# Seven left and seven right operands of the mixing, some moved by multiples of 32 bytes, so that all four pairs of addresses modulo 64 occur

## The chip, the core and the metric

The kernel runs on one NeuronCore of a Trainium2 chip. The time is what the device takes for one execution, in microseconds (us); before the change it is 2311.45 us, the median of two runs (2307.46 and 2315.44 us). A smaller time is better. TensorE (PE in the profile) multiplies: it holds a left (stationary) operand of 128 columns, which a weight load (PEld) brings in, and streams a right (moving) operand of up to 512 columns past it; both are read from the on-chip memory SBUF, and results go to PSUM. VectorE (DVE), ScalarE (ACT) and GpSimd (POOL) do elementwise work, and SyncE (SP) issues most DMA transfers.

## The reference, cut to what matters

A layer norm with modulation, an attention with a compressive memory over four segments, its output projection, a second modulated layer norm, and a two-layer MLP that mixes tokens. The change touches only the last part:

```python
h = _layernorm(x, axis=-1)                                  # (B, S, D)
u = jnp.einsum("bsd,sf->bdf", h, w1) + b1                   # (B, D, F)
u = _gelu(u)
y = jnp.einsum("bdf,fs->bds", u, w2) + b2                   # (B, D, S)
```

with S = 2048 tokens, D = 1024 channels, F = 3584, all in float32.

## The kernel before, in words

The first 1000 us or so are the attention (projections at lines 193 and 201, scores at 466 to 473, values at 495), then comes the output projection (`out_proj`, line 706), whose end overlaps the start of the mixing, and from about 1226 us to the end the mixing runs (`mix`, line 798). It has two matrix products, one with `w1` and one with `w2`.

Each product is cut into **units**, and each unit is a 2x2 block product that is done with seven block products instead of eight (sums and differences of blocks are formed ahead). For a unit, `prepare` (line 753) loads the four weight blocks (`wr`), and forms seven **left operands**, numbered q = 0 to 6. Each is a tile `sp` of 128 partitions x 2 x 512 float32r numbers, that is 4096 bytes in each partition: a high part (a rounded copy, made by ScalarE at line 120) and a low part (the remainder, made by VectorE at line 123). The seven tiles come from one tag with seven places, so each unit uses all seven, and a place is free again when TensorE has used it up.

The seven **right operands** stay in place for many units. `b_tile` (line 682) gives one place for each q, of 12288 bytes: three blocks of 2 x 512 numbers (high and low). In the product with `w1` these hold blocks 0 to 2 of the normed activations (`bA`), and block 3 (`bB`) lies in the tiles that later hold the sums; in the product with `w2` they hold up to three blocks of the hidden activations (`bU`). The product with `w1` has 2 phases x 14 units with 4 blocks, the one with `w2` 5 phases x 8 units with 3, 3, 3, 3 and 2 blocks. `load_b` (line 810) refills the right operands at the end of a phase.

`mix` does, for each q and each block, three matmuls of 128 x 128 by 128 x 512: high by high, high by low, low by high (left part first). They add up in a PSUM bank, and ScalarE (line 803) or VectorE (line 805) adds the result to the sums `cc` (product with `w1`) or `ac` (product with `w2`). So there are 28 units x 7 x 12 = 2352 matmuls in the first product and 2352 in the second, 4704 in all. Every matmul loads its left operand anew.

Where things lie is the sum of the sizes of what was placed before: a tile of 8 floats for each partition is 32 bytes. Three unused tiles of that size stand in the kernel already (`offset` at the head of the constants, `pad` and `pad2` in two pools of the attention). As the built program places them, every operand of the mixing is at an address that is 32 modulo 64; modulo 256 all left and right operands of the mixing and of the output projection are at 224. In the attention's projections, the activations `h` are at 224 modulo 256 and the weights `wv` and `wq` at 160. All blocks and parts inside a tile are multiples of 512 bytes apart, so a tile's address modulo 256 holds for all of it.

The order on each engine is chosen by a scheduler that models times when the kernel is built; PE may take matmuls of one product between those of another, as the two have different PSUM banks.

Of the kernel before, what the change touches and what calls it, by code (L numbers as in the profile page):

```python
# [7 lines left out]
F32 = mybir.dt.float32  # L8
F32R = mybir.dt.float32r
# [9 lines left out]
P = 128  # L19
# [25 lines left out]
def attention_and_mlp(ctx, tc, x, wq, wkv, wo, beta, w1, b1, w2, b2, c, wm_a, wm_b, out):  # L45
# [70 lines left out]
    def split(dst, src, hi_eng, lo_eng):  # L116

        hi, lo = dst[:, 0], dst[:, 1]
        if hi_eng is A:
            A.copy(hi, src)  # L120
        else:
            hi_eng.tensor_copy(hi, src)
        lo_eng.tensor_tensor(lo, src, hi.bitcast(F32), op=ALU.subtract)  # L123
# [482 lines left out]
    for g in range(2, NG):  # L606
        n = 8 * g - 13
# [5 lines left out]
    for j in range(32):  # L613
        n = ML0 + MLS * j
        later(n, lambda j=j: mod_fetch(j), n + 2, lambda r, j=j: mod_late(j, r), "V")
    plan(WO0 - 3, lambda: spread(gaw, 0))
    for i in range(8):
        n = WO0 + WOS * i
# [27 lines left out]
    for q in skp + [late, prj, paw]:  # L646
# [6 lines left out]
    b3, raws, sx = (ctx.enter_context(tc.tile_pool(name=n, bufs=1, side="right", reuse_waits="tile"))  # L653
                    for n in ("b3", "wr", "s1"))
# [15 lines left out]
    NPR = 7  # L670
# [11 lines left out]
    def b_tile(pool, nk, q, name):  # L682
        return pool.tile([P, nk, 2, 512], F32R, tag=f"B{q}", bufs=1, name=f"{name}_{q}")

    bA = [b_tile(b3, 3, q, "bA0") for q in range(NPR)]
    pair_h = {}

    def out_proj(tt):
# [61 lines left out]

    sp = ctx.enter_context(tc.tile_pool(name="sp", bufs=1, reuse_waits="tile"))

    def prepare(weights, nk):


        n = nk * P
        r = raws.tile([P, 4, 512], F32, tag="wr", bufs=2, name="wr")[:, :, 0:n]
        SY.dma_start(r, weights)
        a11, a12, a21, a22 = (r[:, i] for i in range(4))
        s1 = sx.tile([P, 512], F32, tag="s1", bufs=1, name="s1")[:, 0:n]  # L760
        ops = {}

        def operand(q, src):
            ops[q] = sp.tile([P, 2, 512], F32R, tag="sp", bufs=7, name=f"sp{q}")[:, :, 0:n]
            split(ops[q], src, A, V)

        def sum_1():
            V.tensor_tensor(s1, a21, a22, op=ALU.add)
            operand(1, s1)

        def sum_2():
            V.tensor_tensor(a21, a11, a21, op=ALU.subtract)
            V.tensor_tensor(a11, s1, a11, op=ALU.subtract)
            operand(2, a11)

        def sum_4():
            V.tensor_tensor(a12, a12, a11, op=ALU.subtract)
            operand(5, a12)

        return ops, [lambda: operand(0, a11), sum_1, sum_2, lambda: operand(3, a12), lambda: operand(4, a21), sum_4,  # L780
                     lambda: operand(6, a22)]
# [42 lines left out]
    def fourth(name):  # L824

        t = [y_tile(f"{name}_{i}") for i in range(4)]
        return [t[q // 2][:, 2 * (q % 2):2 * (q % 2) + 2].bitcast(F32R) for q in range(NPR)]

    first_unit = prepare(w1[0, 0], 4)
    for f in first_unit[1][:2]:  # L830
        f()
# [28 lines left out]
    def w2_unit(ph, g):  # L860
        k0, nk = sum(KP[:ph]), KP[ph]
        return prepare(w2[g, :, 512 * k0:512 * (k0 + nk)].rearrange("p (b n) -> p b n", b=4), nk)
# [12 lines left out]
    for u, (ph, g) in enumerate(units):  # L875
# [35 lines left out]
        if not last:  # L911
            unit = prepare(w1[units[u + 1]], 4)
# [10 lines left out]
        if ph == 0:  # L923
            SY.dma_start(pcd[g], cc)
            if g == NG1 - 1:
                bA, bB = [nxt[q][0] for q in range(NPR)], [nxt[q][1] for q in range(NPR)]
# [74 lines left out]
```

## Time and profile before

| what | us |
|---|---|
| median of two runs | 2311.45 |
| the two runs | 2307.46, 2315.44 |
| span of the profiled execution, first to last instruction | 2310.5 |
| PE busy in it | 2233.7 (97%) |
| PE busy with the mixing (line 798; bU, bA, bB) | 536.3 + 434.5 + 164.6 |
| DVE busy | 1706.3 (74%) |
| ACT busy | 1105.9 (48%) |

How to read it: the profiled execution has no time of its own beside its span. The span lies 1 us below the median of the runs, and between the two of them, so the sum is made on the span and the 1 us is added. A matmul's duration in the trace (some 390 ns for 512 columns) is longer than the distance from one start to the next, since they overlap; what counts for the time is the distance from start to start. In a row of the timeline that stands for N matmuls in a row, that distance is the row's time less one duration, divided by N - 1.

### The profile page before, as it was taken

The numbers are of one execution on the slowest core, as the hardware profiler recorded it, in microseconds if no ns is written. First come the engines' busy times: TensorE is split into PE (matmuls) and PEld (weight loads), VectorE is DVE, ScalarE is ACT, GpSimd is POOL, SyncE is SP. The second block draws the span as 40 slices with busy tenths as digits, with TensorE's granted clock in tenths as the row PEclk, the third lists the DMA queues.
The fourth block names the chain that finished last, engine by engine and source line by source line (L and its number), as shares of the span: only waits on it lengthen the run. The fifth ranks groups of instructions, "written<-read, shape, count | busy, mean of one in ns | idle before, by whom it ended". The sixth has DMA issues, their size and how long they took to land.

```text
span 2310.5 us, 38455 instructions
## 1 busy us (share of the span) xinstructions
PE 2233.7 (97%) x13866; PEld 1920.3 (83%) x13866; DVE 1706.3 (74%) x3814; ACT 1105.9 (48%) x2018; POOL 724.2 (31%) x835
## 2 busy tenths in 40 slices
PE   8999999999999999988999999999999999999998
PEld 7879888888998888877777888888887888888887
DVE  6667666766776766666988565698889787878787
ACT  5477776665666666644323333443334242424232
POOL 3165565655666766653000000023333000000000
PEclk9989999999999999998999999999999999999999
DMA  6666564687566665663455755566557542414133
GB/s 256 199 171 190 168 176 147 193 253 252 162 204 180 196 182 164 185 202 109 137 196 192 268 222 188 200 228 232 208 203 259 186 140 66 150 56 141 55 119 146
DMA packets 172594, 414.67 MB, mean 179 GB/s; under 512 B 17236, under 2 KB 71540, under 8 KB 163444
## 3 DMA queue, kind: packets, MB, share of 16 engines
q1 hardware_dynamic: 167796, 403.83, 53.6%
q10 hardware_dynamic: 4608, 8.39, 1.0%
q8 instruction: 110, 1.80, 0.3%
q14 instruction: 80, 0.66, 0.1%
HBM read 236.23 MB, written 125.06 MB: 156 GB/s over the span
## 4 chain that ended last, share of the span: by engine, by line
PE 77%; DVE 10%; DMA 6%; ACT 3%; issue 2%; POOL 2%; SPq 1%; ACTq 0%; DVEq 0%; POOLq 0%
PE mx L798 41%; PE nps L193 11%; PE qps L201 8%; PE po L706 5%; PE pv L495 3%; DMA wr<-in_w_dram 1%; DVE ac L805 1%; PE a L466 1%; PE sx L431 1%; DVE bU L123 1%; DMA sk<-nt 1%; DMA x<-in_x_dram 1%; PE sz L431 1%; DVE sp L123 1%; DVE wv L123 1%
## 5 line engine op out<-in xcount | busy, mean ns | idle before, releaser
L798 PE MATMUL mx<-bU,sp 128*128 128x512 f32 x2352 | 536.3, 390 | 4.5 <-DVE ac L805 1.9
L798 PEld LDWEIGHTS mx<-bU,sp 128*128 128x128 f32 x2352 | 440.5, 188 | 99.7 <-DVE sp L123 2.7
L193 PE MATMUL nps<-wv,h 128*128 128x256 f32 x3072 | 437.2, 283 | 1.7 <-ACT wv L120 1.2
L798 PE MATMUL mx<-bA,sp 128*128 128x512 f32 x1764 | 434.5, 391 | 2.5 <-DVE sp L123 2.2
L120 ACT CAST sp<-wr 128x384 fp32r<-128x384 f32 (+2 forms) x408 | 216.8, 545 | 441.4 <-PE mx L798 368.0
L481 POOL TENSOR_TENSOR ph<-p,ph 128x640 f16<-128x640 f32 x256 | 377.6, 1496 | 149.9 <-ACT ph L479 144.1
L193 PEld LDWEIGHTS nps<-wv,h 128*128 128x128 f32 x3072 | 404.2, 189 | 7.8 <-ACT wv L120 1.4
L798 PEld LDWEIGHTS mx<-bA,sp 128*128 128x128 f32 x1764 | 332.6, 189 | 73.8 <-DVE sp L123 3.0
L123 DVE TENSOR_TENSOR sp<-wr,sp 128x384 fp32r<-128x384 f32 (+2 forms) x408 | 258.0, 643 | 35.0 <-ACT sp L120 34.7
L805 DVE TENSOR_TENSOR ac<-mx,ac 128x512 f32<-128x512 f32 x280 | 189.3, 685 | 90.3 <-PE mx L798 89.6
L201 PE MATMUL qps<-h,wq 128*128 128x512 f32 x768 | 202.4, 410 | 0.8 <-DVE r L356 0.8
L706 PE MATMUL po<-wo,ots 128*128 128x512 f32 x768 | 184.6, 400 | 11.9 <-DVE x L709 4.1
L706 PEld LDWEIGHTS po<-wo,ots 128*128 128x128 f32 x768 | 147.6, 194 | 44.7 <-issue 4.3
L432 DVE CUSTOM_DVE_ANT_0 sx<-sx,mask 128x128 f32<-128x128 f32 (+1 forms) x256 | 109.7, 428 | 99.0 <-PE sx L431 96.9
L479 ACT CAST ph<-p 128x1280 f16<-128x1280 f32 x128 | 160.7, 1256 | 37.5 <-POOL p L477 36.2
L201 PEld LDWEIGHTS qps<-h,wq 128*128 128x128 f32 x768 | 146.4, 197 | 31.3 <-PE sx L431 0.8
L798 PE MATMUL mx<-bB,sp 128*128 128x512 f32 x588 | 164.6, 389 | 0.0
L477 POOL TENSOR_SCALAR_AFFINE_SELECT p<-p 128x256 f32<-128x256 f32 x256 | 117.6, 469 | 142.4 <-ACT p L470 70.4
L495 PE MATMUL pv<-vp,ph 128*128 128x97 bf16 (+1 forms) x2560 | 146.2, 204 | 5.0 <-POOL ph L481 1.9
L495 PEld LDWEIGHTS <-ph 128*128 128x128 f16 x2560 | 116.4, 99 | 27.2 <-issue 7.9
L805 DVE TENSOR_TENSOR cc<-mx,cc 128x512 f32<-128x512 f32 x140 | 94.6, 683 | 51.0 <-PE mx L798 48.0
L798 PEld LDWEIGHTS mx<-bB,sp 128*128 128x128 f32 x588 | 110.6, 188 | 23.0
(173 smaller groups left out, 3199.8 us busy)
## 6 DMA issues: line engine op xcount, KB each, us to landing
sk<-sg SPq DMA_DIRECT2D x384, 128.0 KB
wr<-in_w_dram SPq DMA_DIRECT2D x28, 1024.0 KB
wr<-in_w_dram SPq DMA_DIRECT2D x32, 768.0 KB
bstu<-ucd SPq DMA_DIRECT2D x28, 768.0 KB
wsp<-wv SPq DMA_DIRECT2D x32, 512.0 KB
rawm<-in_wm_b_dram SPq DMA_DIRECT2D x32, 512.0 KB
wv<-wsp SPq DMA_DIRECT2D x32, 512.0 KB
pcd<-cc SPq DMA_DIRECT2D x14, 1024.0 KB
```

Source lines behind the costliest of these rows:

```text
L120: A.copy(hi, src)
L123: lo_eng.tensor_tensor(lo, src, hi.bitcast(F32), op=ALU.subtract)
L193: T.matmul(ps[:, aa], h[:, j, 128 * tt:128 * tt + 128], wt[:, i, o:o + 256], start=(n == 0), stop=(n >= 6 * NK - 2), skip_group_check=True)
L201: T.matmul(ps, wt[:, i, o:o + 128], h[:, j], start=(k + n == 0), stop=(3 * k + n == 3 * NK - 1))
L432: marks[4 * t + h - LEADS, "V"] = V.tensor_tensor_reduce(o, o, mask[:, 384 - 128 * i:], 1.0, -3.0e38, op0=ALU.add, op1=ALU.max, accum_out= ...
L477: G.affine_select(w, w, pattern=[[0, 2], [1, 128]], compare_op=ALU.is_ge, fill=0.0, base=0, channel_multiplier=-1)
L479: marks[n, "A"] = A.copy(ph[:, 0], p32)
L481: marks[n, "G"] = G.tensor_tensor(ph[:, 1, c], p32[:, c], ph[:, 0, c], op=ALU.subtract)
L495: T.matmul(pv[:, i, 0:w], ph[:, part, o:o + 128], d["vp"][:, j, h, 0:w], start=(n == 0), stop=(n == 19), skip_group_check=True)
L706: T.matmul(ps, os_[:, i, P * ct:P * ct + P], wop[ct, nh][:, j], start=(n == 0), stop=(n == 3 * NK - 1))
L798: T.matmul(ps, ops[q][:, i, P * k:P * k + P], b[:, j], start=(m == 0 and first), stop=(m == 3 * nk - 1), skip_group_check=True)
L805: V.tensor_tensor(d, ps, d, op=ALU.add)
```

## The change

Unused tiles of 32 bytes are put between some operands. Each right operand is followed by one, but for q = 3 (and the last); each left operand q gets a place of its own (`sp0` to `sp6`, in this order) in place of seven places under one tag, with an unused tile after q = 1 and after q = 4.

```diff
-    bA = [b_tile(b3, 3, q, "bA0") for q in range(NPR)]
+    bA = []
+    for q in range(NPR):
+        bA.append(b_tile(b3, 3, q, "bA0"))
+        if q in (0, 1, 2, 4, 5):
+            b3.tile([P, 8], F32, name=f"gapb{q}")
...
     sp = ctx.enter_context(tc.tile_pool(name="sp", bufs=1, reuse_waits="tile"))
 
+    spt = lambda q: sp.tile([P, 2, 512], F32R, tag=f"sp{q}", bufs=1, name=f"sp{q}")
+    for q in range(NPR):
+        spt(q)
+        if q in (1, 4):
+            sp.tile([P, 8], F32, name=f"gaps{q}")
+
...
         def operand(q, src):
-            ops[q] = sp.tile([P, 2, 512], F32R, tag="sp", bufs=7, name=f"sp{q}")[:, :, 0:n]
+            ops[q] = spt(q)[:, :, 0:n]
             split(ops[q], src, A, V)
```

No instruction of the computation is added, removed or given another size. The addresses in the built program, modulo 64 and (in brackets) modulo 256, and the matmuls of each:

| q | left `sp` | right `bA`, `bU` | matmuls with these | right `bB` | matmuls with `bB` |
|---|---|---|---|---|---|
| 0 | 32 (224) | 0 (64) | 588 | 32 (32) | 84 |
| 1 | 32 (224) | 32 (96) | 588 | 32 (32) | 84 |
| 2 | 0 (0) | 0 (128) | 588 | 32 (32) | 84 |
| 3 | 0 (0) | 32 (160) | 588 | 32 (32) | 84 |
| 4 | 0 (0) | 32 (160) | 588 | 32 (32) | 84 |
| 5 | 32 (32) | 0 (192) | 588 | 32 (32) | 84 |
| 6 | 32 (32) | 32 (224) | 588 | 32 (32) | 84 |

Before, all of these are 32 (224). What lies beyond moves along: the weight blocks `wr` and the sum `s1` go from 32 to 0 modulo 64, the sums `ac` and `cc` stay at 32. The built order of instructions is the same up to the start of the mixing; from there PE, DVE, ACT and SP take the same work in a somewhat different order, since the scheduler now has one place for each q.

## The prediction, on record before the run

> **What bounds the kernel now.** I read the page's first part, then the table of stretches for the mixing's line (798), then PE's timeline inside single stretches.
>
> ```profile
> span 2310.5 us, 38455 instructions
> PE 2233.7 (97%) x13866; PEld 1920.3 (83%) x13866; DVE 1706.3 (74%) x3814; ACT 1105.9 (48%) x2018; POOL 724.2 (31%) x835
> ...
> L798 PE MATMUL mx<-bU,sp 128*128 128x512 f32 x2352 | 536.3, 390 | 4.5 <-DVE ac L805 1.9
> L798 PE MATMUL mx<-bA,sp 128*128 128x512 f32 x1764 | 434.5, 391 | 2.5 <-DVE sp L123 2.2
> L798 PE MATMUL mx<-bB,sp 128*128 128x512 f32 x588 | 164.6, 389 | 0.0
> ```
>
> The three groups are all matmuls of the mixing: 2352 + 1764 + 588 = 4704. PE sat idle before them for 4.5 + 2.5 = 7.0 us in all. PE is thus the bound of the mixing, and with so little idle time any nanosecond that a matmul takes longer is paid at the end of the kernel.
>
> ```profile
> core 0: us, PE busy (x) PEld busy (x), PEclk, DMA share, GB/s
> 1350.00:1750.00 400.00, 400.00 (x1766) 331.32 (x1765) 1.00 0.56 209
> 1810.00:1900.00 90.00, 89.82 (x397) 73.97 (x396) 1.00 0.37 117
> ```
>
> At a granted clock of 1.00, 1766 matmuls start in 400 us: one each 226.5 ns. All operands are alike here (the same address modulo 256), and the spacing is the same in both products (90 / 397 = 226.7 ns).
>
> **What the address pair does in this trace.** The attention's query projection (line 201) has matmuls of the same form, 128 x 128 by 128 x 512 with high and low parts, but left and right lie 64 bytes apart modulo 128. Three rows of PE's timeline, one of the mixing first:
>
> ```profile
> start us, us, engine line op out<-in xcount [idle before <-releaser]
> 1502.12 2.20 PE L798 MATMUL mx<-bA,sp 128*128 128x512 f32 x9
> ...
> 665.57 3.60 PE L201 MATMUL qps<-h,wq 128*128 128x512 f32 x15
> ...
> 240.09 4.13 PE L201 MATMUL qps<-h,wq 128*128 128x512 f32 x17
> ```
>
> Less one duration (0.39, 0.39 and 0.40 us) and divided by one less than the count, the spacings are 226, 229 and 233 ns. No waits lie inside these rows. So the distance between the two operands is the most likely reason why equal matmuls take 2.8 or 6.6 ns longer than 226.5; that the stage differs in other ways (more ACT and POOL work beside it) speaks against it, but the spacing keeps the same value over a whole row while that work comes and goes.
>
> The output projection and the mixing also show what happens when a stream starts anew after a wait: the first matmuls are slower, then the spacing settles.
>
> ```profile
> 2119.50 1.77 PE L798 MATMUL mx<-bU,sp 128*128 128x512 f32 x7
> ...
> 2120.66 1.75 PE L798 MATMUL mx<-bU,sp 128*128 128x512 f32 x7
> ```
>
> The first row comes right after a wait, the second a microsecond later: seven matmuls cost 0.02 us more until they settle.
>
> **The change part by part.**
>
> *The gaps.* By the addresses of the built program, of 4704 matmuls 2604 have left and right at different addresses modulo 64 (q = 0, 3, 4, 5 with bA and bU: 4 x 588 = 2352; q = 2, 3, 4 with bB: 3 x 84 = 252). Another 756 agree modulo 64 but lie 64 apart modulo 128 (q = 6 with bA and bU: 588; q = 0, 1 with bB: 168). The remaining 1344 agree modulo 128, of which 588 have both at 0 (q = 2).
> - The 756 are like the query projection: +2.8 ns (its commoner value) makes 756 x 2.8 = 2.1 us; at +6.6 it is 5.0 us.
> - The 2604 have no like in the trace. From below: +0, or a gain (a rival, below). From above: the left operand's read no longer hidden, 60 ns (a rival, below). The nearest rows are the two of the query projection, and I take the larger, +6.6 ns, since a distance of half a 64-byte step should not fit better than a whole one: 2604 x 6.6 = 17.2 us. At 2.8 it is 7.3 us.
> - The 1344 I cost at nothing: they agree, as all do now.
> - Changes of the pair: in the built order of after, PE goes from one distance modulo 128 to another 645 times, against never before. Each may unsettle the stream as a restart does, 0.02 us: at most 645 x 0.02 = 12.9 us. A stretch between two changes has 4704 / 646 = 7 matmuls on average, and those with bB only three, which is too short to pay it in full: I take half, 6.5 us.
>
> *A place of its own for each q.* The operands are ready long before they are needed, because ACT waits for PE to free a place, not PE for ACT:
>
> ```profile
> engine line waited for: us in total, times, longest us
> ACT sp L120 <- PE mx L798: 440.6, 259, 5.0
> ...
> PE mx L798 <- DVE ac L805: 1.9, 3, 0.9
> PE mx L798 <- DVE sp L123: 1.7, 2, 0.8
> PE mx L798 <- ACT sp L120: 0.6, 1, 0.6
> ```
>
> (The first row is of all engines from 1300 us on, the others of PE from 1262 us on.) Seven places stay seven places, used in the same order; cost nothing. What hides it is the lead of nearly one unit, 84 matmuls x 226.5 ns = 19 us, in the first product; if it were gone, ACT's queue would stop at one place, and behind it the copies of results (line 803) that free PSUM.
>
> *The order at the start of the mixing.* The scheduler begins with three products at once where it had two.
>
> ```profile
> 1226.24 1.25 PE L798 MATMUL mx<-bA,sp 128*128 128x512 f32 x4 [0.28 <-ACT sp L120]
> 1229.71 3.36 PE L798 MATMUL mx<-bA,sp 128*128 128x512 f32 x7 [2.22 <-DVE sp L123]
> ```
>
> Here PE waits once for 2.2 us, and the seven matmuls after it stand (3.36 - 0.39) / 6 = 495 ns apart. Against 226.5 ns that loses 2.2 + 6 x 0.27 = 4 us. Another order may lose it twice or not at all: -4 to +4 us, taken as 0. Line 758's transfers move past others on SP's queue there, by one or two places; they wait for free buffers of wr, not for the queue.
>
> *DVE and ACT at other addresses.* Their tiles move too (wr and s1 to 0 modulo 64), and no row shows them there. DVE is the fuller one:
>
> ```profile
> 1300.00:1600.00 300.00, 300.00 (x1325) 248.51 (x1324) 213.06 (x293) 113.41 (x190) 26.66 (x17) 1.00 0.58 215
> 1600.00:1900.00 300.00, 297.90 (x1310) 245.21 (x1310) 252.20 (x376) 111.20 (x184) 64.27 (x39) 1.00 0.56 201
> ```
>
> (The third number after the window's length is DVE's, with its count.) DVE is busy for 213 and 252 of 300 us, so in the fuller stretch it could become 300 / 252 = 1.19 times as slow before it, and not PE, set the pace. Costed at nothing.
>
> **The sum.** 17.2 + 2.1 + 6.5 = 25.8 us: span 2310.5 + 25.8 = 2336.3, and with the 1 us to the median 2337 us (+1.1%). This case's own range: from 7.3 + 2.1 = 9.4 us (2321) to 17.2 + 5.0 + 12.9 = 35.1 us (2347).
>
> **The rivals.**
>
> *Not slower: a right operand at 0 modulo 64 is read in fewer pieces.* Shorter matmuls of the attention:
>
> ```profile
> 127.75 0.22 PE L472 MATMUL a<-sk 98*128 98x128 f32 x1
> 127.81 0.33 PE L473 MATMUL a<-sk 98*128 98x256 f32 x1
> ...
> 67.98 4.24 PE L193 MATMUL nps<-wv,h 128*128 128x256 f32 x36
> ```
>
> 128 columns take 60 ns, 256 take (4.24 - 0.28) / 35 = 113 ns. In steps of 113 / 17 = 6.65 ns that is 9 and 17 steps for 8 and 16 pieces of 64 bytes, one more than needed, as an operand has that starts in the middle of a piece; all these start at 32 modulo 64. At 0 the step would go: 588 x 3 = 1764 matmuls (q = 0, 2, 5) x 6.65 = 11.7 us less, 2300 us, if the unlike pairs cost nothing. Against it: 512 columns take 34 steps, two more than 32, which a cost in proportion to the length describes as well. It decides from the point where those products' spacing falls under 226 ns.
>
> *Much slower: the two reads get in each other's way all along.* If the streams are half a step apart, each of the nine pieces of a left operand (128 x 4 = 512 bytes, from the middle of a piece) could hold up the right one by half a step: 9 x 3.3 = 30 ns x 2604 = 78 us, 2389 us. The upper bound is a left operand's read not hidden at all, which the 60 ns above limit (a 128-column matmul with its own load): 156 us, 2467 us. It passes 2% from 46 / 2604 = 17.7 ns, a spacing of 244 ns. For it: the spacing of the mixing is as even as if both reads ran in step. Against it: the largest excess of any row here is 6.6 ns.
>
> *The change does nothing to the time.* The spacing follows from the column count alone, and the query projection's 229 and 233 ns come from its stage. The time stays at 2311 us. For it: rows of the same line show both 229 and 233 ns at the same addresses. Against it: both differ from the 226 ns of all rows with like addresses.
> The Trainium skill stands on this rival's side: "SBUF — State Buffer", section "Who interferes with whom", gives TensorE two independent read ports and says "PE and ACT never wait on anyone", and "TensorE: Matmul & The Clock Gate", section "Back-to-back issue gap", gives N / 2.4 + 2.5 ns, 216 ns for 512 columns, with no address in it. The trace does not agree with either in full: 226 ns is the least spacing of any 512-column row here, and 229 and 233 ns occur in equal matmuls without a wait.
>
> **How the numbers follow.** Chances: the sum above 0.45, much slower 0.33, not slower 0.12, nothing 0.10. The predicted time is the first one's, 2337 us. The range 2298 to 2390 us holds the first, the third and the fourth, and about half of the second; outside are the other half of that (0.16) and a little below (0.04). About 2% (46 us) is what a measurement of this kernel can tell from no change. Slower by more: the second case and a tail of the first, 0.34. Faster by more would need 10 ns off each of all 4704 matmuls, for which no row speaks: 0.01. Within 2%: 0.65.
>
> **What would show it.** In PE's timeline of after: spacings of q = 1 and 2 at 226 to 227 ns, of q = 6 at 229 to 233, of q = 0, 3, 4, 5 at 233. Were q = 0, 2 and 5 (with bA or bU) under 226, the first rival is right; were the unlike pairs over 244, the second. PE's idle time before line 798 should stay under 15 us, and DVE's mean for an addition at line 805 should stay at 685 ns:
>
> ```profile
> L805 DVE TENSOR_TENSOR ac<-mx,ac 128x512 f32<-128x512 f32 x280 | 189.3, 685 | 90.3 <-PE mx L798 89.6
> ```
>
> If either changes, the time has gone to the order or to DVE and the reasoning about addresses is not what decides.

## The result, and the profile after

The changed kernel takes 2336.74 us, the median of two runs (2335.95 and 2337.53 us), against 2311.45 us before: 1.0108 times as long, with a 95% interval of 1.0089 to 1.0127. It is slower by 25 us, which is clear of the scatter and under 2%. The prediction said 2337 us. The number is right, but of the terms that it is made of only the largest came out; the experiments show which others did not.

The page of the changed kernel (its line 808 is line 798 of before):

```profile
span 2334.2 us, 38446 instructions
PE 2257.6 (97%) x13866; PEld 1916.6 (82%) x13866; DVE 1709.4 (73%) x3814; ACT 1106.0 (47%) x2018; POOL 722.6 (31%) x835
...
L808 PE MATMUL mx<-bU,sp 128*128 128x512 f32 x2352 | 549.8, 395 | 2.4 <-DVE ac L815 1.7
...
L808 PE MATMUL mx<-bA,sp 128*128 128x512 f32 x1764 | 444.1, 396 | 3.1 <-DVE sp L123 1.9
...
L815 DVE TENSOR_TENSOR ac<-mx,ac 128x512 f32<-128x512 f32 x280 | 190.3, 686 | 96.8 <-PE mx L808 95.9
...
L808 PE MATMUL mx<-bB,sp 128*128 128x512 f32 x588 | 167.9, 394 | 0.2 <-DVE bB L123 0.2
```

The span is 23.7 us longer and PE is busy 23.9 us longer, with the same 13866 matmuls. The three groups of line 808 take 549.8 + 444.1 + 167.9 = 1161.8 us against 1135.4 us, 26.4 us more, and the other groups together 2.5 us less. PE's waits before them are 5.7 us against 7.0, and VectorE's addition stays at 686 ns (685 before). So neither a wait nor VectorE pays, the matmuls themselves do. The table of stretches for this line, with the same stretch as before:

```profile
core 0: us, PE busy (x) PEld busy (x), PEclk, DMA share, GB/s
1350.00:1750.00 400.00, 400.00 (x1720) 322.90 (x1719) 1.00 0.56 207
1850.00:2050.00 200.00, 200.00 (x860) 161.22 (x859) 1.00 0.35 110
```

1720 matmuls start in the 400 us that held 1766: one each 232.6 ns in place of 226.5, at the same granted clock of 1.00.

From the start times of single matmuls in the two traces, put beside the built order (which names q and so the addresses), the spacing by pair follows. Below, the distance is the left operand's address less the right one's, modulo 256; the mean leaves out spacings over 260 ns, which are waits, the one slow spacing after a wait (some 340 ns), and in before a stretch of some 427 ns each at a lower clock; a spacing is put down to the matmul that starts it; the last column is the count times what the mean lies over 226.67 ns.

```
distance   matmuls of after          count  mean ns  over 226.67, us
 96        q 3, 4, 5 with bA, bU     1764   233.7    12.4
160        q 0 with bA, bU            588   233.5     4.0
224        q 2, 3, 4 with bB          252   231.7     1.3
 64        q 6 with bA, bU            588   232.8     3.6
192        q 0, 1 with bB             168   231.7     0.9
128        q 1, 2 with bA, bU        1176   232.2     6.5
  0        q 5, 6 with bB             168   230.8     0.7
                                     4704            29.4
(before: distance 0, all 4704, 226.8 ns, 0.4 us)
```

Of these 29.4 - 0.4 = 29.0 us, 3.6 are given back by shorter stretches over 260 ns (13.1 us before, 9.5 after), and 1.4 as the mixing starts 1.4 us earlier: 24.0, and the span grew by 23.7 us. The time is thus accounted for. Most of the 3.6 us is one stretch: after its longest wait, before has 13 spacings of some 427 ns at a granted clock of 0.51, 13 x 0.2 = 2.6 us, and after has no such stretch. Before, then after:

```profile
1229.80:1236.00 6.20, 6.20 (x15) 4.90 (x16) 0.51 0.16 46
```

```profile
1229.80:1236.00 6.20, 5.98 (x25) 4.44 (x24) 1.00 0.22 54
```

Among the kernels of the experiments below, some with all pairs alike (e3) and some with unlike ones (e6, e9, e10, e12) have such a stretch early in the mixing, and others of both kinds have none. So these 2.6 us are chance as far as the traces tell, and no effect of the distance.

What stands out is that no pair kept its old spacing, not even the 1176 that agree modulo 128.

### The profile page after: what moved, and what is told of

Same layout as the page of the kernel before. It is cut to its first block, busy times and chain, and to the rows that moved or that the text cites. A ratio compares the mean times of both kernels' runs of the same rounds, so it can differ in the third digit from the quotient of the medians.

```text
span 2334.2 us, 38446 instructions
## 1 busy us (share of the span) xinstructions
PE 2257.6 (97%) x13866; PEld 1916.6 (82%) x13866; DVE 1709.4 (73%) x3814; ACT 1106.0 (47%) x2018; POOL 722.6 (31%) x835
## 4 chain that ended last, share of the span: by engine, by line
PE 78%; DVE 8%; DMA 5%; ACT 3%; POOL 3%; issue 2%; SPq 1%; ACTq 0%; DVEq 0%; POOLq 0%
PE mx L808 43%; PE nps L193 11%; PE qps L201 7%; PE po L710 5%; PE pv L495 3%; POOL ph L481 1%; PE a L466 1%; PE sx L431 1%; PE sz L431 1%; DMA x<-in_x_dram 1%; DMA sk<-nt 1%; PE up L413 1%; DMA wr<-in_w_dram 1%; PE a L469 1%; ACT ph L479 1%
## 5 line engine op out<-in xcount | busy, mean ns | idle before, releaser
L808 PE MATMUL mx<-bU,sp 128*128 128x512 f32 x2352 | 549.8, 395 | 2.4 <-DVE ac L815 1.7
L808 PE MATMUL mx<-bA,sp 128*128 128x512 f32 x1764 | 444.1, 396 | 3.1 <-DVE sp L123 1.9
L123 DVE TENSOR_TENSOR sp<-wr,sp 128x384 fp32r<-128x384 f32 (+2 forms) x408 | 264.2, 655 | 35.3 <-ACT sp L120 34.2
L808 PE MATMUL mx<-bB,sp 128*128 128x512 f32 x588 | 167.9, 394 | 0.2 <-DVE bB L123 0.2
```

Source lines behind the costliest of these rows:

```text
L808: T.matmul(ps, ops[q][:, i, P * k:P * k + P], b[:, j], start=(m == 0 and first), stop=(m == 3 * nk - 1), skip_group_check=True)
```

## The experiments

Three theories. **Distance** (called A in the expectations): the distance between left and right sets a steady spacing. **Changes** (called S): only going from one pair to another costs. **Pieces** (called F): a right operand at 0 modulo 64 is read faster. Ratios are to before, on the same chip.

**e1 and e2: one uniform distance of 32 with bA and bU, from either side.** The pairs with bB stay alike.

```diff
+    sp.tile([P, 8], F32, name="lead")       # e1: ahead of the left operands
...
+    b3.tile([P, 8], F32, name="tail")       # e2: after the right operands, which moves bA and bU down
```

> Before, with one unused tile of 32 bytes ahead of all left operands: every left operand is at 0 modulo 256, bA and bU stay at 224, bB moves to 0. So in the product with w2 all 2352 matmuls have one and the same unlike pair (left 0, right 32 modulo 64), with no change of pair. Theory A, that an unlike pair costs 6.6 ns steadily: spacing of bU 233 ns, and 4116 matmuls with bU and bA x 6.6 = 27 us, about 2339 us. Theory S, that only changes of the pair cost: spacing of bU 226.5 ns as before, and only the product with w1, which changes between bA and bB, pays some 6 to 12 us, about 2320 us. Theory F, that a right operand at 0 modulo 64 is read faster: nothing gained here, as the right operands with bA and bU stay, about 2311 us.

> Before, with one unused tile of 32 bytes after all right operands, which moves bA and bU to 192 modulo 256 (0 modulo 64); left operands and bB stay at 224. The mirror image of the run with the left operands at 0, at the same distance of 32 between left and right. Theory A: spacing of bU 233 ns, about 2339 us. Theory S: bU at 226.5 ns, about 2320 us. Theory F: 4116 matmuls x 6.65 ns less, spacing of bU 220 ns, about 2284 us.

Measured: e1 2339.94 us (1.0113, interval 1.0091 to 1.0135), e2 2337.76 us (1.0104, 1.0085 to 1.0123). The stretch from 1850 us, in the product with `w2`, of before, of e1, then of e2:

```profile
1850.00:2050.00 200.00, 199.82 (x882) 165.07 (x881) 1.00 0.35 111
```

```profile
1850.00:2050.00 200.00, 200.00 (x859) 161.01 (x858) 1.00 0.35 110
```

```profile
1850.00:2050.00 200.00, 200.00 (x858) 160.92 (x857) 1.00 0.34 108
```

Both start some 858 matmuls in 200 us, one each 233 ns, where before had 882 with a short wait among them. From the single starts, the mean with bU is 233.3 ns in both, and the same repeating row of 231, 232 and 235 ns. There is no change of pair in this product, so Changes falls as the main cause. In e2 the right operands are at 0 modulo 64 and no faster, so Pieces falls. Which of the two is moved makes no difference.

**e3: all operands at 0 modulo 256.**

```diff
+    sp.tile([P, 8], F32, name="lead")
...
+    b3.tile([P, 56], F32, name="tail")
```

> Before, with 32 bytes ahead of the left operands and 224 bytes after the right ones: all left operands, bA, bU and bB are at 0 modulo 256. All pairs are alike, as before, only at 0 in place of 32 modulo 64. Theory A (the distance decides): spacing 226.5 ns, about 2311 us. Theory S (changes decide): the same. Theory F (a right operand at 0 is read faster): 4704 x 6.65 = 31 us less, spacing 220 ns, about 2280 us.

Measured: 2312.65 us (0.9999, 0.9984 to 1.0015).

```profile
1350.00:1750.00 400.00, 400.00 (x1766) 331.24 (x1765) 1.00 0.55 210
```

The count is that of before to the matmul. 0 and 32 modulo 64 are equally good as long as left and right agree modulo 256.

**e4: places of their own, no gaps.** The changed kernel without its seven gap tiles.

```diff
-        if q in (0, 1, 2, 4, 5):
-            b3.tile([P, 8], F32, name=f"gapb{q}")
...
-        if q in (1, 4):
-            sp.tile([P, 8], F32, name=f"gaps{q}")
```

> After without any gap: each left operand has a place of its own, with the order of work that follows from it, and all addresses are those of before. Theories A, S and F all say 2311 us. The rival that the new order or the fixed places cost the time says up to 2337 us, with PE waits before line 798's matmuls of more than 15 us.

Measured: 2316.29 us (1.0009, 0.9993 to 1.0024), which is no difference that can be told; the spacing with bU is 226.8 ns. The other half of the edit, with the order that follows from it, is not the cause.

**e5 and e6: distances of 64 and 128 with bA and bU.** As e1, with `[P, 16]` and `[P, 32]`.

> Before, with 64 bytes ahead of the left operands: left at 32 modulo 256, bA and bU at 224, so every pair in them agrees modulo 64 but lies 64 apart; no change of pair in the product with w2. Theory D64 (only the distance modulo 64 counts): spacing of bU 226.5 ns, about 2312 us. Theory D128 or D256 (the distance counts modulo 128 or 256): 229 to 233 ns as in the query projection, 4116 x 2.8 to 6.6 = 12 to 27 us, 2323 to 2339 us.

> Before, with 128 bytes ahead of the left operands: left at 96 modulo 256, bA and bU at 224, 128 apart. D64 and D128: spacing of bU 226.5 ns, about 2312 us. D256: 233 ns, about 2339 us. In the changed kernel q = 1 and 2 lie 128 apart and run at 232 ns in their short stretches; if they settle at 226.5 here, their cost there came from the changes of pair, and if not, from the distance itself.

Measured: e5 2337.88 us (1.0108, 1.0088 to 1.0129), e6 2336.51 us (1.0106, 1.0087 to 1.0125). Stretches of e5, then of e6:

```profile
1350.00:1750.00 400.00, 400.00 (x1721) 323.06 (x1720) 1.00 0.55 205
1850.00:2050.00 200.00, 200.00 (x859) 161.47 (x858) 1.00 0.33 107
```

```profile
1350.00:1750.00 400.00, 400.00 (x1728) 324.60 (x1727) 1.00 0.55 205
1850.00:2050.00 200.00, 200.00 (x862) 162.07 (x861) 1.00 0.34 107
```

With bU, 233.3 ns at 64 and 232.4 ns at 128. So neither agreement modulo 64 nor modulo 128 is enough. The 232.2 ns of q = 1 and 2 in the changed kernel is what distance 128 costs for good, not an effect of the changes around them.

**e7: like and unlike pairs in turn.** e4 with one gap of 32 bytes after q = 3, so that with bU q = 0 to 3 are at distance 0 and q = 4 to 6 at 32.

```diff
     for q in range(NPR):
         spt(q)
+        if q == 3:
+            sp.tile([P, 8], F32, name="gap")
```

> The kernel with a place for each left operand and no gap, with one gap of 32 bytes after q = 3: with bU, q = 0 to 3 have like pairs (distance 0) and q = 4 to 6 a distance of 32, so the pair changes between stretches of 6 to 9 matmuls. If a change costs nothing, the like pairs stay at 226.5 ns and the unlike run at 233 ns, 2100 x 6.6 = 14 us, about 2328 us. If each change unsettles the stream, the like pairs lie at 229 to 232 ns too, 3 to 5 ns on 2604 matmuls = 8 to 13 us more, about 2340 us.

Measured: 2331.61 us (1.0085, 1.0067 to 1.0104), between the two expectations.

```profile
1850.00:2050.00 200.00, 200.00 (x870) 163.08 (x869) 1.00 0.35 111
```

From the single starts: bU at distance 0 runs at 228.2 ns, at 32 at 232.9; bA at distance 0 at 230.1. By place in a stretch at distance 0, the first eight spacings after a change have means of 228 to 232 ns, and from the ninth on it is 226.7 to 227.1. Added up, a change to distance 0 costs some 25 ns, close to the 0.02 us of a restart in the prediction. At distance 32 no such settling shows: the mean by place is 231 to 235 ns from the first spacing to the last. So in these traces a change costs only where there is a better spacing to settle into. The changed kernel agrees: at 96, 160, 64 and 128 with bA and bU its means are 233.7, 233.5, 232.8 and 232.2 ns, and without changes of pair (bU in e9, e10, e5 and e6) they are 234.3, 233.3, 233.3 and 232.4.

**e8: alike pairs in the attention's projections.** Before, with `pad2` larger:

```diff
-    acst.tile([P, 8], F32, name="pad2")
+    acst.tile([P, 24], F32, name="pad2")
```

> Before, with the unused tile pad2 of the attention 96 bytes in place of 32: the projection weights wv and wq move by 64 to 224 modulo 256, where the activations h are, so the projections' pairs become alike; the mixing stays as it was. If the distance decides there too, query projection rows settle at 226.5 ns in place of 229 and 233 and key/value rows at 113 in place of 113 to 118: at most 768 x 4 + 3072 x 2.5 = 11 us less, about 2300 us, and less where short stretches do not settle. If the stage and not the distance makes those rows slow: no change, 2311 us.

Measured: 2313.01 us (1.0001, 0.9991 to 1.0010). Its query projection and its key/value projection:

```profile
666.04 3.11 PE L201 MATMUL qps<-h,wq 128*128 128x512 f32 x13
```

```profile
69.57 4.24 PE L193 MATMUL nps<-wv,h 128*128 128x256 f32 x34
```

The queries settle at (3.11 - 0.39) / 12 = 227 ns, where before had 229 and 233: the distance decides there as well. But key/value, with 256 columns, now takes (4.24 - 0.28) / 33 = 120 ns where before had 113, at distance 64. What fits 512 columns does not fit 256. Over all key/value matmuls (spacings over 140 ns left out) the mean rises from 116.1 to 119.4 ns, some 10 us, and the queries give back one. Of these 9 us only 2.3 reach the start of the mixing (1228.51 us against 1226.24): PE's spacings over 260 ns ahead of it add up to 5.3 us less in this profile, and the rest is not accounted for. The kernel's time does not change, so this half of the expectation, the gain, is missed.

**e9 to e12: the other distances.** The same two edits in one kernel each, the lead ahead of the left operands 96, 160, 192 or 224 bytes and `pad2` 64, 128, 160 or 224.

```diff
+    sp.tile([P, 24], F32, name="lead")      # e9; e10: 40, e11: 48, e12: 56
...
-    acst.tile([P, 8], F32, name="pad2")
+    acst.tile([P, 16], F32, name="pad2")    # e9; e10: 32, e11: 40, e12: 56
```

> Two distances at once, left less right modulo 256: 96 in the mixing with bA and bU (96 bytes ahead of the left operands); in the projections, by pad2 of 64 bytes, 32 for key/value (256 columns) and 224 for queries (512 columns). If 0 is the only distance that fits for 512 columns, bU runs at 232 to 234 ns and the time is about 2338 us plus or minus what the projections change. If distances over 64 fit again, 226.5 ns. Key/value rows: 113 ns at 64 and some 119 ns at 0 so far; an unlike distance modulo 64 should be no better than 119, up to 10 us more for the kernel.

> Distance 160 in the mixing with bA and bU; in the projections, by pad2 of 128 bytes, 224 for key/value and 32 for queries. If 0 is the only distance that fits: bU at 232 to 234 ns, about 2338 us. If the distance counts the same both ways round, bU has the pattern and mean of distance 96. Query rows: 233 ns as in the mixing at 32.

> Distance 192 in the mixing with bA and bU, which is the query projection's own distance in the kernel before; in the projections, by pad2 of 160 bytes, 192 for key/value and 64 for queries. If the distance alone sets the spacing, bU shows the query projection's two values, 229 or 233 ns: 2352 + 1764 matmuls x 2.5 to 6.7, 2321 to 2339 us. Key/value: if 192 is to 256 columns what 64 is, 113 to 118 ns.

> Distance 224 in the mixing with bA and bU, 32 the other way round; in the projections, by pad2 of 224 bytes, 128 for key/value and for queries. If the distance counts the same both ways round, 233.3 ns as at 32, about 2339 us; if the order matters (the left operand read ahead of the right one), another value, 226.5 ns at the least. Key/value at 128: 113 ns if 64 fits because it is not 0, 119 ns if as at 0.

Measured: e9 2340.50 us (1.0117, 1.0100 to 1.0134), e10 2340.42 us (1.0124, 1.0104 to 1.0144), e11 2327.11 us (1.0059, 1.0037 to 1.0081), e12 2343.17 us (1.0120, 1.0096 to 1.0144). These times hold the changed projections as well, so the distances are compared by spacing. Two stretches of e11, and a row of its timeline:

```profile
1900.00:1950.00 50.00, 50.00 (x215) 40.50 (x216) 1.00 0.41 127
...
2150.00:2200.00 50.00, 50.00 (x220) 41.00 (x220) 1.00 0.20 64
```

```profile
2219.65 4.74 PE L799 MATMUL mx<-bU,sp 128*128 128x512 f32 x20
```

At distance 192 the mixing has the query projection's two values: 215 matmuls in 50 us are 233 ns, and the row of 20 is (4.74 - 0.39) / 19 = 229 ns. Another stage, other work beside it, the same distance, the same two values. All distances from the single starts, with bU for the mixing, and for the two projections the mean from the ninth matmul of a stretch on:

```
distance (left less right, modulo 256)     0     32     64     96    128    160    192    224
mixing, 512 columns, ns                226.8  233.3  233.3  234.3  232.4  233.3  229.9  233.3
queries, 512 columns, ns               227.2  233.3  233.3      -  232.6      -  229.6  233.3
key/value, 256 columns, ns             119.9  118.4  114.1      -  118.9      -  117.6  117.0
kernel                                before     e1     e5     e9     e6    e10    e11    e12
(key/value: 0 is e8, 32 e9, 64 before, 128 e12, 192 e11, 224 e10)
(queries: 0 is e8, 32 e10, 64 e11, 128 e12, 192 before, 224 e9)
```

The queries run in another stage, and their distance was set by another tile (`pad2`); at all six distances that were tried there, the two rows agree within 0.4 ns (at 192 both are means over the two values). So it is the distance and not the stage that sets the spacing for 512 columns.

It is not the same both ways round (64 and 192 differ), and of the eight distances 0 alone leaves 512 columns at 226.8 ns. For 256 columns 64 is the best of six. None of the twelve runs is faster than before beyond its interval.

## Why the prediction was right, and where it was not

- **Where it is bound.** PE sets the time of the mixing, and a longer spacing is paid in full: 29.0 us of spacing, less 3.6 us of spacings over 260 ns and 1.4 us of an earlier start, became 23.7 us of span.
- **Unlike pairs modulo 64, 17.2 us.** Right: they cost 12.4 + 4.0 + 1.3 = 17.7 us. The mechanism taken from the query projection's rows, that the two addresses' distance sets the spacing, is shown by e1, e2, e3, e8 and e11. The choice of 6.6 ns over 2.8 by a 64-byte step landed without its reason: 32, 64, 160 and 224 all cost 6.5 ns, whole step or half, and the 2.8 is one of two values at 192 alone.
- **The 756 that are 64 apart modulo 128, 2.1 us.** Mis-sized: 3.6 + 0.9 = 4.5 us. I took the query projection as their like, but it lies at 192 modulo 256; at 64, where the 588 of q = 6 are, there is no state of 229 ns (e5: 233.3). The 168 with bB do lie at 192, but ran at 231.7.
- **The 1344 that agree modulo 128, costed at nothing.** Wrong: 6.5 + 0.7 = 7.2 us. Agreement modulo 128 is not enough, e6, and the sign that q = 1 and 2 would run at 226 to 227 ns failed: they ran at 232.2. The addresses modulo 256 stood in the working, but before the run every pair was at one of two distances, 0 and 64 modulo 128, and I took the smaller modulus for granted.
- **Changes of the pair, 6.5 us.** Wrong as a term of its own. Settling is real (e7) but costs only on the way to distance 0, where the changed kernel has 168 of 4704 matmuls; going between unlike pairs adds nothing that can be told to their own spacing (e7).
- **Places, order, VectorE at nothing.** Right within what e4 can tell (0.9993 to 1.0024), and by VectorE's 686 ns. One reading there is off: the 495 ns at the start of the mixing subtracts a duration of 0.39 us, but at the clock of 0.51 a single matmul lasts 0.63 us (the row at 1232.86 us), which makes (3.36 - 0.63) / 6 = 455 ns.

So the 26 us came out by a cancellation, and that is luck: 6.5 us too much for changes, 10.1 us too little for the spacings (0.5 + 2.4 + 7.2, of which 0.7 are the 168 alike pairs that do not settle), and 5 us given back by the shorter stretches over 260 ns and the earlier start. With the right rule the sum is simpler: nearly all of the 4704 matmuls are 5 to 7 ns longer, which is why four pairs mixed (1.0108) cost the same as a single uniform shift (e1, 1.0113).

Of the rivals, **pieces** is refuted by e2 and e3, **much slower** by all runs (no distance exceeds 234.3 ns), and **nothing** by e1, whose only edit is a shift. The Trainium skill, quoted there with "SBUF — State Buffer", "Who interferes with whom", calls TensorE's two read ports independent. Here a uniform shift of one operand lengthens the spacing by 2.9%, from 226.8 to 233.3 ns (e1), so the addresses of the two reads do not act independently on the time; whether one read waits for the other is not shown. The 216 ns that the prediction takes from the Trainium skill, "TensorE: Matmul & The Clock Gate", "Back-to-back issue gap", is given there for an isolated matmul and not for a steady stream.

What stays open is the mechanism. That the two reads meet in some part of the memory chosen by address bits below 256 fits all rows, but no run here looks into it. Why one distance has two states, and why 256 columns prefer 64, is not explained. Distances that are not multiples of 32 bytes were not tried.

## What to carry to other kernels

Where 512-column float32r matmuls with a new left operand each run back to back, read the distance from start to start, not the duration, and compare it between stages: equal matmuls at unequal spacing, without a wait and at the same granted clock, may point to addresses, and shifting one operand tells. Place left and right operands at the same address modulo 256 for 512 columns; a stray 32-byte tile ahead of one of them cost 3% of each such matmul. Measure another column count by itself, and do not count on a rule of a smaller modulus because all pairs at hand agree in it.

## What the runs showed of the hardware that I had not expected

- The spacing depends on the distance modulo 256, and 256 rather than 512 is the period where it could be seen: in before the left operands and bA are 256 apart modulo 512, in e3 they agree modulo 512, and both run at 226.8 ns. The same holds at 32, 64 and 128: modulo 512 these are 288, 320 and 384 in the mixing and 32, 64 and 128 for the queries, and the spacings agree within 0.2 ns.
- A distance may have two steady states: at 192, long stretches at 228.9 and others at 233.3 ns, within one kernel and at the same addresses (e11). With bU no other distance showed a second one.
- The penalty is no share of the length: from the best distance to the usual slow one it is 6.5 ns for 512 columns (226.8 to 233.3), and from the best to the worst 5.8 ns for 256 (114.1 to 119.9).
